# Keys of rows 2 and 3: the last half chunk as 64-row matmul pairs in a joint visit

## The chip, the cores and the metric

The kernel runs on one core of a Trainium2 chip. The metric is the time of one execution on the device in microseconds (us), as the median of several executions. "PE" is the tensor engine, "PEld" its weight loads, DVE the vector engine, ACT the scalar engine, POOL the GpSimd engine and SP the sync engine that issues most transfers.

## The reference

Two branches read the same x (2048 tokens, 448 features) and are mixed by a gate per token:

```python
qkv = x @ wqkv                       # 16 heads of 28
phi(t) = concat(softmax(t @ w_phi), softmax(-(t @ w_phi)))   # for q and k
kv, z = phi(k)^T v, sum phi(k)
a = (phi(q) kv / (phi(q) z + 1e-6)) @ wo
b = gelu(x @ w1 + b1) @ w2 + b2
out = g * a + (1 - g) * b            # g = sigmoid(sum(x * gate_w))
```

What matters here is the keys, `x @ Wpk`, where Wpk is the key weight already multiplied by w_phi. The 448 features are three chunks of 128 and half a chunk of 64.

## The kernel before

`xT` holds x transposed: features on partitions, tokens along the row. A tile is 128 tokens, a key pair (the "row" of the change's name) is two tiles. The fourth chunk is loaded as features 320 to 447, and the weight is zero in the first 64 partitions of that chunk. So it is a full 128-row matmul for 64 useful features:

```python
def k_pair(u, b1=False):                 # keys of tiles 2u, 2u+1
    pk = four("pk")
    for i in range(2):
        for c in range(NC4):             # 4 chunks, the last one half empty
            nc.tensor.matmul(pk[:, i, 0:D], lhsT=xT[:, c, tile], rhs=Wpk[:, c, :], ...)
    if b1:                               # a tiny matmul that turns b1 onto partitions
        nc.tensor.matmul(pk[:, 1, 480:480 + NJ], lhsT=b1c, rhs=ident[:, 0:NJ], ...)
    k_exp(u, pk)                         # two exponentials on ACT, PSUM -> phik
    if b1: nc.scalar.copy(out=b1T[:], in_=pk[:, 1, 480:480 + NJ])

# order                                   # POOL copies
k_pair(0); k_pair(1); k_norm(0)           # WvS <- WvG, halves swapped (2 copies)
k_pair(2); k_norm(1)                      # WkS[0:64]   <- Wpk[64:128]
k_pair(3, b1=True)                        # WkS[64:128] <- Wpk[0:64]
v_both()                                  # x1o <- xT[64:128, 3, 512:1024]
for g in range(NG): q_pair(g, 0)
for r in range(4): k_two(r); v_two(r); ...; q_pair(r, 1)
```

The values of rows 2 and 3 (`v_both`) avoid the waste already: their last chunk is computed from two places at once, one tile from partitions 0 to 63 (through the shifted copies `x1o` and `WvS`), the other from partitions 64 to 127. `k_two` does all its chunks so. For that it reads `xS`, a copy of x with the partition halves swapped, which transfers fill (`swap_x`). `four()` hands out PSUM buffers, three in turn plus a fourth.

The softmax here doesn't subtract the row's maximum and nothing guards it: scores larger than these inputs give would overflow.

Of the kernel before, what the change touches and what calls it, by code (L numbers as in the profile page):

```python
# [13 lines left out]
D = 448  # L14
# [3 lines left out]
P = 128  # L18
# [10 lines left out]
HP = 64  # L29
# [6 lines left out]
def kernel(  # L36
# [14 lines left out]
    nc = tc.nc  # L51
# [9 lines left out]
    def pair(name):  # L61
        return ps.tile([P, 2, 512], F32, name=name, tag="pair", bufs=3)

    def wide(name):
        return ps.tile([P, 2, 512], F32, name=name, tag="acc", bufs=1)
# [3 lines left out]
    def four(name):  # L69
        turn[0] += 1  # L70
        return wide(name) if turn[0] % 4 == 0 else pair(name)


    xT = consts.tile([P, NC4, S], BF16, name="xT")
# [23 lines left out]
    WvG = attn.tile([P, NC4, D + 1], BF16, name="WvG")  # L98
    WvS = attn.tile([P, NC4, D + 1], BF16, name="WvS")
    WkS = attn.tile([P, NC4, D], BF16, name="WkS")  # L100
    Wpk = attn.tile([P, NC4, D], BF16, name="Wpk")
# [38 lines left out]
    def swap_x(h, part=None):  # L140
        ev = slice(2 * h * 512, 2 * h * 512 + 512)
        od = slice(2 * h * 512 + 512, 2 * h * 512 + 1024)
        if part != "odd":
            nc.sync.dma_start(xS[0:HP, :, h, :], xT[HP:P, :, ev])
        if part != "even":
            nc.sync.dma_start(xS[HP:P, 0:3, h, :], xT[0:HP, 0:3, od])
# [29 lines left out]
                          in_=mask[:, PW:PW + 2, None].to_broadcast([P, 2, DH]))  # L176
    nc.gpsimd.memset(KVbd[:], 0.0)
    for g in range(NG):
        nc.gpsimd.tensor_copy(
            out=KVbd[:, g].rearrange("p s (i w) -> p s i w", i=2)[:, :, :, KW - 2:KW],  # L180
            in_=m4[:, None, :, :].to_broadcast([P, 2, 2, 2]))
# [11 lines left out]
    def copy(on_act, out, in_):  # L193
        if on_act:
            nc.scalar.copy(out=out, in_=in_)
        else:
            nc.vector.tensor_copy(out=out, in_=in_)  # L197

    def v_out(u, v_ps, tiles, on_act=False):
        copy(on_act, vaug[:, 2 * u:2 * u + 2, :, 0:PW],  # L200
             v_ps[:, :, 0:D].rearrange("p i (x d) -> p i x d", x=NPR))
        copy(on_act, lg[:, tiles], v_ps[:, :, D])
# [7 lines left out]
                                 rhs=WvG[:, c, :], start=(c == 0), stop=(c == NC4 - 1))  # L210
        v_out(u, v_ps, slice(2 * u, 2 * u + 2), on_act)

    def v_both():
        vs = [four("v_ps"), four("v_ps")]
        for m in range(2):
            for i in range(2):
                t = 4 + 2 * m + i
                for c in range(3):
                    nc.tensor.matmul(vs[m][:, i, 0:D + 1], lhsT=xT[:, c, t * P:(t + 1) * P],  # L219
                                     rhs=WvG[:, c, :], start=(c == 0), stop=False)  # L220
        for i in range(2):
            nc.tensor.matmul(vs[0][:, i, 0:D + 1], lhsT=x1o[:, i * P:(i + 1) * P],  # L222
                             rhs=WvS[0:HP, 3, :], start=False, stop=True)
            nc.tensor.matmul(vs[1][:, i, 0:D + 1], lhsT=xT[HP:P, 3, (6 + i) * P:(7 + i) * P],
                             rhs=WvG[HP:P, 3, :], start=False, stop=True)
        for m in range(2):
            v_out(2 + m, vs[m], slice(4 + 2 * m, 6 + 2 * m))

    def prep(W_T, out_at, engines):
        for m in range(2):  # L230
# [33 lines left out]
    def k_exp(u, pk):  # L264
        tt = slice(2 * u, 2 * u + 2)
        src = pk[:, :, 0:D].rearrange("p i (x w) -> p i x w", w=PW)
        nc.scalar.activation(out=phik[:, tt, :, 0, 0:PW], in_=src, func=ACT.Exp)  # L267
        nc.scalar.activation(out=phik[:, tt, :, 1, 0:PW], in_=src, func=ACT.Exp, scale=-1.0)  # L268

    def k_norm(u):  # L270
        tt = slice(2 * u, 2 * u + 2)
        sums = work.tile([P, 32, 2], F32, name="sums", bufs=3)
        ph = phik[:, tt].rearrange("p t x s w -> p (t x s) w")[:, :, 0:PW]
        ph = ph.rearrange("p y (h d) -> p y h d", d=DH)
        nc.vector.reduce_sum(out=sums[:], in_=ph, axis=AX.X)  # L275
        rec = work.tile([P, 32, 2], F32, name="rec", bufs=3)
        nc.vector.reciprocal(out=rec[:], in_=sums[:])  # L277
        parts = [(nc.gpsimd, 0, 32)] if u < 7 else [(nc.vector, 0, 16), (nc.gpsimd, 16, 32)]
        for eng, lo, hi in parts:
            eng.tensor_tensor(out=ph[:, lo:hi], in0=ph[:, lo:hi],  # L280
                              in1=rec[:, lo:hi, :, None].to_broadcast([P, hi - lo, 2, DH]),
                              op=ALU.mult)

    def k_pair(u, b1=False):
        pk = four("pk")
        for i in range(2):
            t = 2 * u + i
            for c in range(NC4):
                nc.tensor.matmul(pk[:, i, 0:D], lhsT=xT[:, c, t * P:(t + 1) * P],  # L289
                                 rhs=Wpk[:, c, :], start=(c == 0), stop=(c == NC4 - 1))  # L290
        if b1:
            nc.tensor.matmul(pk[:, 1, 480:480 + NJ], lhsT=b1c, rhs=ident[:, 0:NJ],
                             start=True, stop=True, skip_group_check=True)
        k_exp(u, pk)
        if b1:
            nc.scalar.copy(out=b1T[:], in_=pk[:, 1, 480:480 + NJ])
# [89 lines left out]
    def swap_w(W_S, W):  # L386
        nc.sync.dma_start(W_S[0:HP, :, :], W[HP:P, :, :])
        nc.sync.dma_start(W_S[HP:P, 0:3, :], W[0:HP, 0:3, :])

    def swap_on_pool(W_S, W):  # L390
        nc.gpsimd.tensor_copy(out=W_S[0:HP, :, :], in_=W[HP:P, :, :])
        nc.gpsimd.tensor_copy(out=W_S[HP:P, 0:3, :], in_=W[0:HP, 0:3, :])

    nc.gpsimd.dma_start(b1c[0:NJ, :], B_b1.rearrange("(j p) -> j p", p=P))
    x1o = oT[0:HP, 1, 0:512]
    swap_on_pool(WvS, WvG)
    swap_on_pool(WkS, Wpk)
    nc.gpsimd.tensor_copy(out=x1o, in_=xT[HP:P, 3, 512:1024])
    swap_x(0, "even")
    swap_w(WqS, Wpq)  # L400
    swap_x(0, "odd")
# [9 lines left out]
    nc.sync.dma_start(wo_sb[64:65, 3, :], B_b2[None, :])  # L411

    k_pair(0)
    k_pair(1)
    k_norm(0)
    k_pair(2)
    k_norm(1)
    k_pair(3, b1=True)
    v_both()
    nc.sync.dma_start(w2_sb[:], B_w2.rearrange("(j p) n -> p j n", p=P))  # L420
    k_norm(2)
# [148 lines left out]
```

## Time and profile before

| | kernel before |
|---|---|
| median of the first three runs | 155.75 us (155.66 to 155.77) |
| span of the profiled execution | 153.4 us |
| PE busy | 149.4 us, 97% |
| first key matmul to first query matmul | 8.87 us (11.13 to 20.00) |

PE is busy without a gap from the weight preparation to its last matmul, 2.95 us before the end, so the time is the sum of PE's matmuls, plus any wait for something with a date of its own. The prediction shows the lines.

### The profile page before, as it was taken

To read this page: it belongs to the slowest core of one execution; us is meant where nothing else is said; L and a number is where in the kernel's file an instruction comes from. 1 tells how busy PE (TensorE), PEld (TensorE's weight loads), DVE (VectorE), ACT (ScalarE), POOL (GpSimd) and SP (SyncE) were. 2 spreads that over 40 slices of the span, in tenths; PEclk is the share of its full clock that TensorE was granted. 3 is DMA by queue.
4 is the path that set the end of the run, shared out by engine and by line. 5 is a ranking of instruction groups with operands and counts; after the bars stand their busy time and mean duration, and the time that the engine had idled before them with its cause. 6 is when DMAs were issued, how large, how long until landed. Compare 5 with 4: busy or idle time off the path is not lost.

```text
span 153.4 us, 3189 instructions
## 1 busy us (share of the span) xinstructions
PE 149.4 (97%) x1302; PEld 79.8 (52%) x1302; DVE 83.0 (54%) x244; ACT 77.3 (50%) x93; POOL 39.8 (26%) x41
## 2 busy tenths in 40 slices
PE   7999999999999999999999999999999999999992
PEld 2675544444544854444444455555556555555561
DVE  3444989499890050000000059999977999977100
ACT  2569949999889437676777740111311111111112
POOL 7999796949874000000000000000000000000000
PEclk9999999999999999999999999999999999999999
DMA  4996998999990000000000001124332123334411
GB/s 149 235 214 150 215 168 195 231 221 218 232 368 23 4 0 4 0 0 4 0 0 0 4 0 34 34 44 93 94 94 64 41 64 91 74 94 38 109 45 30
DMA packets 27922, 14.11 MB, mean 92 GB/s; under 512 B 19842, under 2 KB 27780, under 8 KB 27908
## 3 DMA queue, kind: packets, MB, share of 16 engines
q1 hardware_dynamic: 26692, 13.25, 38.9%
q10 hardware_dynamic: 1152, 0.65, 1.6%
q8 instruction: 10, 0.16, 0.5%
q14 instruction: 4, 0.03, 0.1%
q0 software_dynamic: 64, 0.01, 0.0%
HBM read 6.11 MB, written 1.84 MB: 52 GB/s over the span
## 4 chain that ended last, share of the span: by engine, by line
PE 97%; ACT 0%; issue 0%; DVE 0%; ACTq 0%
PE y L509 28%; PE hp L450 28%; PE y L515 8%; PE pq L324 8%; PE nm L465 4%; PE pk L289 4%; PE v_ps L308 3%; PE pk L316 3%; PE acc L335 2%; PE v_ps L209 2%; PE warm_ps L371 2%; PE v_ps L219 2%; PE w_ps L236 1%; PE xp L354 1%; PE v_ps L222 0%; ACT res L518 0%
## 5 line engine op out<-in xcount | busy, mean ns | idle before, releaser
L509 PE MATMUL y<-w_sb,gel 128*128 128x448 bf16 (+2 forms) x238 | 45.2, 341 | 0.0
L450 PE MATMUL hp<-xT,w_sb 64*128 64x512 bf16 x196 | 42.6, 376 | 0.0
L450 PE MATMUL hp<-xS,w_sb 64*128 64x512 bf16 x196 | 42.6, 376 | 0.0
L455 ACT ACTIVATE gel<-hp,b1T 128x1024 bf16<-128x1024 f32 x28 | 30.8, 1111 | 13.0 <-PE hp L450 13.0
L518 ACT ACTIVATE res<-y,ungate 128x448 bf16<-128x448 f32 (+2 forms) x17 | 10.4, 612 | 50.3 <-PE y L515 50.1
L509 PEld LDWEIGHTS <-gel 128*128 128x128 bf16 x238 | 22.6, 98 | 19.6
L450 PEld LDWEIGHTS <-w_sb 64*128 64x128 bf16 x392 | 19.0, 94 | 23.0
L280 POOL TENSOR_TENSOR phik<-phik,rec 128x1792 bf16<-128x1792 bf16 (+1 forms) x8 | 24.9, 3128 | 6.5 <-DVE rec L277 6.5
L470 DVE COPY st<-nm 128x32 f32<-128x32 f32 x32 | 4.5, 183 | 35.6 <-PE nm L465 35.6
L486 DVE TENSOR_TENSOR tmp<-nm,al 128x448 bf16<-128x448 f32 x32 | 18.4, 615 | 0.0
L275 DVE TENSOR_REDUCE sums<-phik 128x64 f32<-128x1792 bf16 x8 | 16.0, 2000 | 2.7 <-ACT phik L268 2.7
L515 PE MATMUL y<-wo_sb,oT 128*128 128x448 bf16 (+2 forms) x68 | 14.7, 342 | 0.0
L324 PE MATMUL pq<-xT,Wpq 64*128 64x512 bf16 x56 | 12.9, 376 | 0.0
L324 PE MATMUL pq<-xS,WqS 64*128 64x512 bf16 x56 | 12.9, 376 | 0.0
L329 ACT ACTIVATE EqP<-pq 128x1024 bf16<-128x1024 f32 x8 | 8.4, 1049 | 3.8 <-PE pq L324 3.8
L197 DVE CAST vaug<-v_ps 128x896 bf16<-128x896 f32 x7 | 7.5, 1081 | 4.7 <-PE v_ps L209 2.1
L330 ACT ACTIVATE EqN<-pq 128x1024 bf16<-128x1024 f32 x8 | 8.4, 1052 | 0.0
L465 PE MATMUL nm<-KVbd,EqP 128*128 128x120 bf16 x64 | 8.3, 216 | 0.0
L465 PE MATMUL nm<-KVbd,EqN 128*128 128x120 bf16 x64 | 8.3, 216 | 0.0
L267 ACT ACTIVATE phik<-pk 128x896 bf16<-128x896 f32 x8 | 7.7, 957 | 0.3 <-PE pk L289 0.3
L515 PEld LDWEIGHTS <-oT 128*128 128x128 bf16 x68 | 6.0, 98 | 3.5
L268 ACT ACTIVATE phik<-pk 128x896 bf16<-128x896 f32 x8 | 7.7, 967 | 0.0
(102 smaller groups left out, 160.7 us busy)
## 6 DMA issues: line engine op xcount, KB each, us to landing
w_sb<-in_B_w_dram SPq DMA_DIRECT2D x4, 784.0 KB, 11.4
out_dram<-res SPq DMA_DIRECT2D x15, 112.0 KB, 1.9
w_sb<-in_B_w_dram SPq DMA_DIRECT2D x1, 1568.0 KB, 17.1
xS<-xT SPq DMA_DIRECT2D x2, 256.0 KB
oT<-in_A_x_dram ACTq DMA_DIRECT2D x1, 448.0 KB, 3.2
xS<-xT SPq DMA_DIRECT2D x2, 192.0 KB, 3.0
wo_sb<-in_A_wo_dram SPq DMA_DIRECT2D x1, 336.0 KB
WqS<-Wpq SPq DMA_DIRECT2D x1, 256.0 KB, 3.2
```

What stands on the lines that cost most here:

```text
L275: nc.vector.reduce_sum(out=sums[:], in_=ph, axis=AX.X)
L280: eng.tensor_tensor(out=ph[:, lo:hi], in0=ph[:, lo:hi], in1=rec[:, lo:hi, :, None].to_broadcast([P, hi - lo, 2, DH]), op=ALU.mult)
L324: nc.tensor.matmul(pq[:, i, :], lhsT=w_half(Wpq, WqS, i, k)[:, g * P:(g + 1) * P], rhs=x_half(i, k, h), start=(k == 0), stop=(k == NK - 1))
L329: nc.scalar.activation(out=EqP[:, g, dst], in_=src, func=ACT.Exp)
L330: nc.scalar.activation(out=EqN[:, g, dst], in_=src, func=ACT.Exp, scale=-1.0)
L450: nc.tensor.matmul(hp[:, i, :], lhsT=w1_sb[i * HP:(i + 1) * HP, k, j * P:(j + 1) * P], rhs=x_half(i, k, h), start=(k == 0), stop=(k == NK ...
L455: nc.scalar.activation(out=gel[h][:, j, :], in_=hp[:].rearrange("p a b -> p (a b)"), func=ACT.Gelu_apprx_tanh, bias=b1T[:, j:j + 1])
L465: nc.tensor.matmul(nm[s][:, g * 2 * KW:(g + 1) * 2 * KW], lhsT=E[:, g, tok], rhs=KVbd[:, g, s, :], start=True, stop=True)
L486: nc.vector.tensor_tensor(out=tmp[:, s, :].rearrange("p (x h d) -> p x h d", x=NPR, h=2), in0=nmv[s][:, :, 0:PW].rearrange("p x (h d) -> p ...
L509: nc.tensor.matmul(y, lhsT=gel[t // 8][:, j, (t % 8) * P:(t % 8 + 1) * P], rhs=w2_sb[:, j, cols], start=(j == 0), stop=False)
L515: nc.tensor.matmul(y, lhsT=oT[:, c, tok], rhs=wo_sb[:, c, cols], start=False, stop=(c == NC4 - 1))
L518: nc.scalar.activation(out=res[:, cols], in_=y, func=ACT.Copy, scale=ungate[:, t:t + 1])
```

## The change

The intent is to let the keys of rows 2 and 3 do what the values of these rows do: 12 full-row matmuls and two concurrent pairs of 64-row ones, in place of 16 full-row ones. Both rows' buffers must then be open together, so it is a visit of its own (`k_both`). The b1 matmul moves to the second key pair. On POOL the copy of x that the pairs need is moved ahead of the key weight's second half.

```diff
-    def v_both():
-        vs = [four("v_ps"), four("v_ps")]
+    def both(name, W, W_S, n):
+        pair_ps = [four(name), four(name)]
         for m in range(2):
             for i in range(2):
                 t = 4 + 2 * m + i
                 for c in range(3):
+                    nc.tensor.matmul(pair_ps[m][:, i, 0:n], lhsT=xT[:, c, t * P:(t + 1) * P],
+                                     rhs=W[:, c, :], start=(c == 0), stop=False)
         for i in range(2):
+            nc.tensor.matmul(pair_ps[0][:, i, 0:n], lhsT=x1o[:, i * P:(i + 1) * P],
+                             rhs=W_S[0:HP, 3, :], start=False, stop=True)
+            nc.tensor.matmul(pair_ps[1][:, i, 0:n], lhsT=xT[HP:P, 3, (6 + i) * P:(7 + i) * P],
+                             rhs=W[HP:P, 3, :], start=False, stop=True)
+    # v_both() and k_both() call both() and evict (cut)
@@
-    swap_on_pool(WkS, Wpk)
+    nc.gpsimd.tensor_copy(out=WkS[0:HP, :, :], in_=Wpk[HP:P, :, :])
     nc.gpsimd.tensor_copy(out=x1o, in_=xT[HP:P, 3, 512:1024])
+    nc.gpsimd.tensor_copy(out=WkS[HP:P, 0:3, :], in_=Wpk[0:HP, 0:3, :])
@@
     k_pair(0)
-    k_pair(1)
+    k_pair(1, b1=True)
     k_norm(0)
-    k_pair(2)
+    k_both()
     k_norm(1)
-    k_pair(3, b1=True)
     v_both()
```

More of the change, by code (lines that the diff above doesn't have):

```diff
@@ L218, in v_both, with k_both @@
                 for c in range(3):
-                    nc.tensor.matmul(vs[m][:, i, 0:D + 1], lhsT=xT[:, c, t * P:(t + 1) * P],
-                                     rhs=WvG[:, c, :], start=(c == 0), stop=False)
+                    nc.tensor.matmul(pair_ps[m][:, i, 0:n], lhsT=xT[:, c, t * P:(t + 1) * P],
+                                     rhs=W[:, c, :], start=(c == 0), stop=False)
         for i in range(2):
-            nc.tensor.matmul(vs[0][:, i, 0:D + 1], lhsT=x1o[:, i * P:(i + 1) * P],
-                             rhs=WvS[0:HP, 3, :], start=False, stop=True)
-            nc.tensor.matmul(vs[1][:, i, 0:D + 1], lhsT=xT[HP:P, 3, (6 + i) * P:(7 + i) * P],
-                             rhs=WvG[HP:P, 3, :], start=False, stop=True)
-        for m in range(2):
-            v_out(2 + m, vs[m], slice(4 + 2 * m, 6 + 2 * m))
+            nc.tensor.matmul(pair_ps[0][:, i, 0:n], lhsT=x1o[:, i * P:(i + 1) * P],
+                             rhs=W_S[0:HP, 3, :], start=False, stop=True)
+            nc.tensor.matmul(pair_ps[1][:, i, 0:n], lhsT=xT[HP:P, 3, (6 + i) * P:(7 + i) * P],
+                             rhs=W[HP:P, 3, :], start=False, stop=True)
+        return pair_ps
+    def v_both():
+        for m, v_ps in enumerate(both("v_ps", WvG, WvS, D + 1)):
+            v_out(2 + m, v_ps, slice(4 + 2 * m, 6 + 2 * m))
+    def k_both():
+        for m, pk in enumerate(both("pk", Wpk, WkS, D)):
+            k_exp(2 + m, pk)
     def prep(W_T, out_at, engines):
```

## The prediction

> **What bounds the kernel now.** I read the page first, then the chain of work that ended last in order of time, then the timelines of the tensor engine, its weight loads, ACT, POOL and the DMA issues between 11 and 31 us, which is where the diff acts and where its effects meet the next stage.
>
> ```profile
> PE 149.4 (97%) x1302; PEld 79.8 (52%) x1302; DVE 83.0 (54%) x244; ACT 77.3 (50%) x93; POOL 39.8 (26%) x41
> PE 97%; ACT 0%; issue 0%; DVE 0%; ACTq 0%
> ...
> 11.30 6.05 PE pk L289 x32
> 17.35 0.01 PE pk L292
> 17.36 2.31 PE v_ps L219 x12
> 19.67 0.29 PE v_ps L222
> ...
> 20.16 6.04 PE pq L324 x56
> 26.21 1.32 PE pk L316 x14
> ```
>
> The first two lines are busy times and shares of the chain by engine: 97% of the chain is matmul. The rest is that chain in time (start, length, what). The keys of rows 0 to 3 are the 32 matmuls at L289, 6.05 us or 0.189 us each. The values of rows 2 and 3 follow (L219, then half-row pairs L222/L224), then the queries (L324), then the first key visit of the upper half (L316). No gap on PE: each matmul taken out is worth 0.189 us, **unless** something later is waiting for a date that PE doesn't set.
>
> So I looked for such dates. Start, length, engine, line, what it does, from the timelines:
>
> ```profile
> 12.66 1.68 POOL L391 COPY WkS<-Wpk 64x1792 bf16<-64x1792 bf16 x1
> 14.38 1.30 POOL L392 COPY WkS<-Wpk 64x1344 bf16<-64x1344 bf16 x1
> 15.74 0.61 POOL L398 COPY oT<-xT 64x512 bf16<-64x512 bf16 x1
> ...
> 19.24 0.25 ACT L296 COPY b1T<-pk 128x14 f32<-128x14 f32 x1
> 21.72 1.02 ACT L329 ACTIVATE EqP<-pq 128x1024 bf16<-128x1024 f32 x1 [2.22 <-PE pq L324]
> ...
> 19.60 0.09 PEld L222 LDWEIGHTS <-oT 64*128 64x128 bf16 x1 [0.37 <-issue]
> ...
> 23.10 0.59 SPq L146 DMA_DIRECT2D xS<-xT  x1
> DMA to landing us min/median/max: 2.8/2.8/2.8
> ...
> 25.83 0.09 PEld L316 LDWEIGHTS <-xT 64*128 64x128 bf16 x1
> 25.93 0.21 PEld L316 LDWEIGHTS <-xS 64*128 64x128 bf16 x2
> ...
> 30.00 0.09 PEld L316 LDWEIGHTS <-xT 64*128 64x128 bf16 x1
> 30.00 0.31 PEld L316 LDWEIGHTS <-xS 64*128 64x128 bf16 x2
> ```
>
> The last six lines matter most. The second partition swap of x (issued at 23.10, landing 2.8 us later, so at 25.9) fills the half of xS that the first upper-half key visit loads as weights. In the steady visits (30.00) the xT load and the xS load start together. In the first visit the xS load starts 0.10 later, at 25.93, just after the landing. The matmuls lost almost nothing (26.04 and 26.05), since a weight is loaded about 0.2 us ahead. PE meets this transfer **with no slack at all**.
>
> **What the Trainium skill says.** (1) "TensorE: Matmul & The Clock Gate", section "Wait — 56ns, not 53.3ns?": warm back-to-back matmuls start N / 2.4 GHz + about 2.5 ns apart. For 448 columns that is 189 ns; the trace has 6.05 / 32 = 0.189 us. It agrees. The durations of 352 ns in the trace are not the price. (2) Same page, "Part 3: Packing small matmuls — row/col tiling": matmuls in different row groups run concurrently. The trace agrees: L222 and L224 both start at 19.61 and again both at 19.81. (3) "TensorEngine Tiling (Array Packing)", section "Key Properties": "Mode switching requires drain". The trace agrees: before L222 the weight load sat idle for 0.37 us, and the first pair starts at 19.61 although the last full-row matmul started at 19.32 (19.13 + 0.19) and the next slot was 19.51. So entering half-row mode cost 0.10 us. Leaving it is seen where L450 hands over to the 128-row L335: last pair at 50.06, slot 0.216, due at 50.28, started at 50.37, so 0.09 us. (4) "DMA: Bandwidth & Descriptors", section "Why a DMA increments its semaphore by 16 and not by 1": a transfer is done when all its engines have reported. The trace agrees so far as it shows a consumer released 0.03 us after the landing.
>
> **The change part by part.**
>
> Tensor engine. The keys of rows 2 and 3 (tiles 4 to 7) are 16 full-row matmuls now: 16 x 0.189 = 3.02 us. Afterwards there are 12 full-row ones (three whole chunks for four tiles), 12 x 0.189 = 2.27, and four half-row ones in two concurrent pairs, 2 x 0.19 = 0.38. The visit of the values that follows begins with full-row matmuls, so both switches are paid: 0.10 to enter and 0.09 to leave. Sum 2.84. Saved on PE: 3.02 - 2.84 = **0.18 us**; of the ideal two slots, 0.38, half goes into switches. The 64-row form suffices because the last chunk of the weight is zero in its first 64 partitions, by the kernel's own memset. The b1 matmul (14 columns, about 0.03 us of chain) only moves from the fourth key pair to the second.
>
> POOL. The same three copies in another order: 1.68, then 0.61 for the x half (from 14.38 to about 15.0), then 1.30 (to about 16.3). The end is the same as now (16.35), so the first normalise on POOL at 17.39 keeps its date. The new pairs need the first copy and the x half at about 14.15 + 12 x 0.189 = 16.4; they are there at 15.0, 1.4 us early. In the old order the x half would be there only at 16.35, with no slack: that is what the reorder is for. The third copy is needed at 26.
>
> b1. Its DMA is issued by POOL at 9.0 and lands 3.1 us later, at 12.1; the matmul that reads it will now stand at about 14.1 rather than 17.2. Two us to spare.
>
> ACT. The exponentials of pairs 0 and 1 run until 16.05, then the b1T copy (0.25) until 16.3. Pair 2 can now start only when the joint visit is done, about 17.2, where it started at 16.05; so pairs 2 and 3 end about 20.5 rather than 19.2. ACT has the room: it idled 2.22 us before the first query exponential (21.72). Buffers: the second query group needs the buffer of pair 3 at about 21.3, and has it at about 20.5. The first query group needs that of pair 2 at 19.8, and has it at 18.8. No PE wait follows.
>
> The sum at the next date. PE reaches the first upper-half key visit 0.18 us earlier, so its xS load would be due at about 25.65. The landing doesn't move with PE: the swap is issued when the transposed loads of x have landed, those are issued by the sync queue behind swaps that depend on weight preparation before 13 us, and none of that is touched. So the load again starts at 25.93 and its matmul at about 26.03 or 26.05. PE waits 0.16 to 0.18 us there, and the gain is **0.00 to 0.02 us**. After that visit the chain is the same instructions at full PE occupancy, so the rest keeps its length.
>
> **The rivals.** *Gain stays whole.* If in a typical execution the swap lands 0.2 us earlier against PE than in this trace, the 0.18 us come through: 155.57 us. For it: one trace is one draw of DMA timing; against it: the page's DMA row shows the DMA engines nearly always busy up to there, so little makes them earlier. *ACT becomes the bound.* ACT is continuous from 21.72 to 34 us, with 1.8 us per query group against 1.51 on PE, and it starts that stretch from idle; if the later exponentials ran into it, query groups would wait for buffers and the time rise by up to 0.3, to 156.0. Against it: 20.5 is still 1.0 us before the first query result. *A switch costs more than I read off.* If each were 0.2 us, the joint key visit would save nothing; the result is 155.75 again, not distinguishable from the DMA by time but plainly so in the trace. *DVE or POOL late:* the third and fourth normalise start at 22.34 and 24.85, well after the exponentials; I give that no weight.
>
> **Range and chances.** From 155.75 I take 0.05: the central estimate of the DMA case (0.01) mixed with about one chance in four that the swap lands early enough to let 0.18 through. That is 155.70 us. The three runs of the kernel before spread over 0.11 us, and two builds may differ by something like that for no reason in the diff; so 155.40 to 155.95. A change of 2% is 3.1 us; all parts together are a tenth of that, so "same" is nearly certain.
>
> **What would show it.** Right, if in the changed kernel's trace (a) the stretch from the first full-row matmul of the joint key visit to the first of the values' visit is about 2.84 us; (b) the query groups start about 0.18 us earlier, near 19.8; (c) the first xS weight load of the upper half is still at about 25.9, with a wait before it of about 0.2 us and its releaser a DMA; (d) later stages, as the first gelu layer matmul (42.72) and the end, have the old dates. Wrong, if the first xS load moves forward by the whole 0.18, or if PE waits for POOL at the first pair or for ACT at a query group.

## The result, and the profile after

The changed kernel took 155.45 us (median of 6 runs, 155.13 to 155.64), the kernel before 155.70 us in the same rounds and the earlier ones (6 runs, 155.43 to 155.83). The ratio is 0.9983, with a 95% interval of 0.9970 to 0.9996.

The page of the changed kernel, busy times and then the engines' shares of the last chain:

```profile
PE 148.8 (97%) x1302; PEld 78.6 (51%) x1302; DVE 83.1 (54%) x244; ACT 77.4 (50%) x93; POOL 39.6 (26%) x41
PE 91%; DMA 3%; SPq 2%; issue 0%; DVE 0%; ACT 0%; ACTq 0%
```

The number of matmul instructions is the same, since four full-row ones became four half-row ones. The 3% of DMA in the chain is at the start: in this execution the weight preparation met a late transfer of the query weights, at 10.2 us. That is before the changed part. The chain of waits in order of time (start, length, what):

```profile
11.29 3.03 PE pk L296 x16
14.32 0.01 PE pk L299
14.33 2.29 PE pk L219 x12
16.61 0.29 PE pk L222
...
17.10 2.40 PE v_ps L219 x12
...
19.99 6.04 PE pq L331 x56
26.03 1.32 PE pk L323 x14
```

Against the lines of before: the query groups (L331, formerly L324) begin at 19.99 instead of 20.16, and the first upper-half key visit (L323, formerly L316) at 26.03 instead of 26.21. The 0.17 us is there, and it isn't lost at that visit. The timelines of the changed kernel, for PE, its weight loads, POOL, ACT and the transfer issues:

```profile
14.18 2.43 PE L219 MATMUL pk<-Wpk,xT 128*128 128x448 bf16 x12
16.55 0.36 PE L222 MATMUL pk<-WkS,oT 64*128 64x448 bf16 x1
16.75 0.35 PE L222 MATMUL pk<-WkS,oT 64*128 64x448 bf16 x1
17.03 2.47 PE L219 MATMUL v_ps<-WvG,xT 128*128 128x449 bf16 x12
...
17.03 2.03 PEld L219 LDWEIGHTS <-xT 128*128 128x128 bf16 x12 [0.37 <-issue]
...
14.16 0.61 POOL L405 COPY oT<-xT 64x512 bf16<-64x512 bf16 x1
...
17.13 0.92 ACT L274 ACTIVATE phik<-pk 128x896 bf16<-128x896 f32 x1 [0.88 <-PE pk L224]
21.54 1.02 ACT L336 ACTIVATE EqP<-pq 128x1024 bf16<-128x1024 f32 x1 [1.07 <-PE pq L331]
...
22.72 0.59 SPq L146 DMA_DIRECT2D xS<-xT  x1
DMA to landing us min/median/max: 2.8/2.8/2.8
...
25.66 0.09 PEld L323 LDWEIGHTS <-xT 64*128 64x128 bf16 x1
25.66 0.31 PEld L323 LDWEIGHTS <-xS 64*128 64x128 bf16 x2
```

The joint visit is 17.03 - 14.18 = 2.85 us instead of 3.02. The weight loads pause for 0.37 us on leaving the half-row mode, as they do on entering it. ACT starts the third pair's exponentials at 17.13 instead of 16.05 and still idles 1.07 us before the first query group. The swap was issued at 22.72, not at 23.10, and landed at 25.5 instead of 25.9. The xS load was not held up.

### The profile page after: what moved, and what is told of

It reads as the page before. It is cut to its first block, busy times and chain, and to the rows that moved or that the text cites. A ratio compares the mean times of both kernels' runs of the same rounds, so it can differ in the third digit from the quotient of the medians.

```text
span 153.2 us, 3189 instructions
## 1 busy us (share of the span) xinstructions
PE 148.8 (97%) x1302; PEld 78.6 (51%) x1302; DVE 83.1 (54%) x244; ACT 77.4 (50%) x93; POOL 39.6 (26%) x41
## 4 chain that ended last, share of the span: by engine, by line
PE 91%; DMA 3%; SPq 2%; issue 0%; DVE 0%; ACT 0%; ACTq 0%
PE hp L457 28%; PE y L516 28%; PE y L522 8%; PE pq L331 8%; PE nm L472 4%; PE v_ps L315 3%; PE pk L323 3%; DMA WqT<-in_A_wqkv_dram 3%; PE acc L342 2%; PE pk L296 2%; SPq L138 2%; PE v_ps L219 2%; PE pk L219 1%; PE w_ps L243 1%; SPq L126 1%; PE v_ps L222 0%
## 5 line engine op out<-in xcount | busy, mean ns | idle before, releaser
L331 PE MATMUL pq<-xT,Wpq 64*128 64x512 bf16 x56 | 12.9, 376 | 0.0
L331 PE MATMUL pq<-xS,WqS 64*128 64x512 bf16 x56 | 12.9, 376 | 0.0
```

The lines of the kernel that those rows point to most:

```text
L331: nc.tensor.matmul(pq[:, i, :], lhsT=w_half(Wpq, WqS, i, k)[:, g * P:(g + 1) * P], rhs=x_half(i, k, h), start=(k == 0), stop=(k == NK - 1))
```

## The experiments

The theory after this result was: the pairs save two slots of 0.189 us (a slot is the time from the start of one matmul to the next) less one switch into half-row mode and one out, and the date of the swap is a draw of each execution (a matter of chance) that mostly leaves room. The rivals were: the regrouping or the POOL order brings the gain; the new order itself moves the swap; the switches cost nothing and something else limits the gain. All results below were correct. They were taken on three chips: the second look of the changed kernel, full rows, the order and the old POOL order on one, the late and early swaps on another, and the rest on a third. Each set was compared with runs of the kernel before in the same rounds.

The next table is made from the profiles. "Stretch" is the start of the first query matmul less that of the first key matmul. "Due" is the start of the first upper-half xT weight load, with which the xS load starts when nothing holds it. "Landing" is the date in the trace at which the second swap's second half had reported completely. All in us.

| profile | first key matmul | stretch | due | landing | xS load |
|---|---|---|---|---|---|
| before | 11.13 | 8.87 | 25.83 | 25.89 | 25.93 |
| before, second look | 10.99 | 8.87 | 25.69 | 25.43 | 25.69 |
| full rows in the joint visit | 11.15 | 8.86 | 25.84 | 25.75 | 25.85 |
| only the order changed | 11.39 | 8.91 | 26.12 | 26.13 | 26.18 |
| two visits | 10.99 | 8.91 | 25.73 | 25.64 | 25.73 |
| old POOL order | 10.88 | 8.82 | 25.53 | 25.42 | 25.53 |
| changed | 11.13 | 8.70 | 25.66 | 25.49 | 25.66 |
| changed, second look | 11.31 | 8.74 | 25.88 | 25.82 | 25.88 |
| changed, third look | 10.77 | 8.70 | 25.30 | 25.44 | 25.48 |
| rows 0 and 1 too | 11.45 | 8.53 | 25.81 | 25.95 | 25.99 |

In all ten, the first xS matmul starts 6.05 us after the first query matmul: PE lost nothing at the swap in any of them. What follows, to the end of PE's work, is equal within 0.01 us as well. So up to the end of PE's work, profiles of these kernels differ in two numbers only: when the first key matmul starts (10.77 to 11.45, set by the stages before it) and the stretch. After PE's last matmul come 2.94 to 2.96 us more in nine of them, and 3.32 us in "rows 0 and 1 too". The stretch of one kernel repeats within 0.04 us: in the second look of the changed kernel and in "only the order changed", the fourth key matmul starts 0.23 us after the third instead of 0.19.

### The changed kernel again, second and third look

> The changed kernel once more, for a second draw of its transfers and more timed runs. Theory (the two slots less two switches are saved on PE, and come through when the second swap of x lands before PE wants it): PE again reaches the first query matmul near 19.83 us if the weight preparation ends at the same date; the ratio to the kernel before is between 0.9983 and 1.000, nearer 0.9988 (0.18 us of 155.7). If the landing is later than about 25.65 in this profile, a wait of PE before the first xS weight load takes its place. Rival (the new order itself moved the transfers earlier, worth another 0.1 us or more): the landing is again at about 25.5 and not near 25.9.

> The changed kernel for a third time, beside the two above. Theory: stretch from the first key matmul to the first query matmul 8.70 to 8.74 us, no wait at the first xS load, ratio 0.9988 within the interval. The start of the key visit (11.13 and 11.31 us in the earlier two profiles) sets the rest of the difference between executions.

The second set gave 155.40 us against 155.37 (ratio 0.9993, interval 0.9977 to 1.0009), the third 155.47 against 155.41 (0.9997, 0.9981 to 1.0013). Each interval holds both 0.9989, which 0.17 us would make, and 1.000. The mean of the three ratios is 0.9991, or 0.14 us. The stretch was 8.74 and 8.70. The rival "the new order moves the swap" falls: the landing was at 25.82 in the second look. The third look tells more. The weight loads of the changed kernel in its third look, then its matmuls at that place:

```profile
25.30 0.09 PEld L323 LDWEIGHTS <-xT 64*128 64x128 bf16 x1
25.48 0.12 PEld L323 LDWEIGHTS <-xS 64*128 64x128 bf16 x2
...
25.51 0.35 PE L323 MATMUL pk<-Wpk,xT 64*128 64x448 bf16 x1
25.51 0.54 PE L323 MATMUL pk<-WkS,xS 64*128 64x448 bf16 x2
```

PE came early (first key matmul at 10.77), and the swap, landing 0.14 us after the xS load was due, held that load for 0.18 us. The two matmuls start at 25.51 all the same, where the steady pace puts them. A matmul that starts 0.03 us after its weight load began is enough, so almost the whole lead of 0.21 us of the loads is slack.

### The kernel before, second look

> The kernel before, for a second look. Theory: stretch 8.87 to 8.91 us. The landing of the second swap in the first profile (25.89, just 0.04 us before the load that needs it) was a late draw: the load is now due at least 0.05 us after the landing. Rival (the kernel before always meets it exactly): within 0.05 us again.

One run, 155.32 us; it serves for its dates alone. The transfer issue and the weight loads of the kernel before in its second look:

```profile
22.66 0.59 SPq L146 DMA_DIRECT2D xS<-xT  x1
...
25.69 0.09 PEld L316 LDWEIGHTS <-xT 64*128 64x128 bf16 x1
25.69 0.31 PEld L316 LDWEIGHTS <-xS 64*128 64x128 bf16 x2
```

The swap went out at 22.66 instead of 23.10 and landed 0.26 us before it was wanted. The theory's condition holds: the late landing isn't a property of the kernel before. Whether the first look differs by the execution alone or also by its chip is not shown, since the kernel before was not profiled twice on one chip. On the chip of the second look of the changed kernel, the landing came 14.51 to 14.74 us after the first key matmul in four kernels.

### Full rows in the joint visit

```diff
-        for m, pk in enumerate(both("pk", Wpk, WkS, D)):
+        # as k_pair: all four chunks on 128 rows, for both pairs, then the exponentials
+        for m in range(2):
+            for i in range(2):
+                for c in range(NC4): nc.tensor.matmul(pks[m][:, i, 0:D], ..., rhs=Wpk[:, c, :])
```

> The joint visit of the keys of rows 2 and 3, but with all 16 matmuls on full rows; everything else as in the changed kernel. Theory: the gain is the half-row pairs alone, so this is 0.17 to 0.20 us slower than the changed kernel on PE: joint visit 3.02 us, first query matmul near 20.0, ratio to the kernel before 1.000. Rival (the regrouping, the b1 move or the order of copies gives the gain): ratio near 0.998 and the first query matmul near 19.83.

155.63 us against 155.37, ratio 1.0014 (0.9999 to 1.0028). The chain of waits of this kernel:

```profile
14.35 3.04 PE pk L238 x16
17.39 2.30 PE v_ps L219 x12
```

The visit takes 3.04 us and the stretch is back at 8.86. Visit, order and b1 move are as in the changed kernel; only the pairs are gone, and the gain with them.

### Only the order changed

```diff
     k_norm(0)
-    k_both()
+    k_pair(2)
     k_norm(1)
+    k_pair(3)
     v_both()
```

> The kernel before with only the new order of POOL copies and the b1 matmul moved to the second key pair. Theory: nothing on PE's chain changes, first query matmul near 20.0, ratio 1.000. Rival (POOL's new order shifts the swap transfers): landing of the second swap near 25.5 rather than 25.9, and ratio below 0.9995.

155.52 us against 155.37, ratio 1.0008 (0.9994 to 1.0022). The stretch is 8.91 and the landing at 26.13, the latest of all. Neither the copies' new order nor the b1 move helps, and they don't bring the swap forward.

### The old POOL order

```diff
-    nc.gpsimd.tensor_copy(out=WkS[0:HP, :, :], in_=Wpk[HP:P, :, :])
+    swap_on_pool(WkS, Wpk)
     nc.gpsimd.tensor_copy(out=x1o, in_=xT[HP:P, 3, 512:1024])
-    nc.gpsimd.tensor_copy(out=WkS[HP:P, 0:3, :], in_=Wpk[0:HP, 0:3, :])
```

> The changed kernel with POOL's copies in the old order, so that the x half is copied last and ready at about 16.35 us, where PE's first half-row load wants it at about 16.45 to 16.55. Theory: no wait or one of under 0.1 us; ratio to the kernel before 0.9985 to 0.9995, first query matmul 19.83 to 19.95. Rival (the reorder is what makes the change work): PE waits 0.2 us or more before the first half-row pair, first query matmul at 20.0 or later, ratio 1.000 or above.

155.23 us against 155.37, ratio 0.9989 (0.9973 to 1.0004), so the time tells nothing. The trace does. POOL's last copy and PE's first half-row weight load with the old order:

```profile
15.76 0.61 POOL L405 COPY oT<-xT 64x512 bf16<-64x512 bf16 x1
...
16.42 0.09 PEld L222 LDWEIGHTS <-oT 64*128 64x128 bf16 x1 [0.49 <-POOL oT L405]
```

The load starts 0.05 us after the copy ends and waited 0.49 us instead of the 0.37 of a bare switch. The stretch is 8.82: 0.12 us of the 0.17 is given back. That is a little over the 0.1 us that the theory allowed and under the 0.2 of the rival. PE was early here (10.88) while POOL's dates hardly moved, so by these dates the amount would be smaller where PE starts later; in the changed kernel the copy ends at 14.77, some 1.8 us early.

### Two visits, one pair each

```diff
-    k_both()
+    k_split(2)      # 6 full-row matmuls, then one half-row pair (tiles 4 and 5)
     k_norm(1)
+    k_split(3)      # the same for tiles 6 and 7
```

> The half-row pairs in two visits, one pair each (tiles 4 and 5, then tiles 6 and 7), so that PE enters and leaves the half-row mode twice for the same two slots saved; the copies that the first pair needs come first on POOL. Theory (a switch in and out costs 0.19 us together, as much as one slot): the stretch from the first key matmul to the first query matmul is 8.70 + 0.19 = 8.89 us, no better than the 8.87 of the kernel before; ratio 1.000. Rival (a switch is hidden, and the gain of 0.17 us is limited by something else): 8.70 us or less, ratio 0.999.

155.64 us against 155.41, ratio 1.0013 (0.9999 to 1.0028). PE's timeline with two visits:

```profile
14.04 1.29 PE L237 MATMUL pk<-Wpk,xT 128*128 128x448 bf16 x6
15.27 0.36 PE L239 MATMUL pk<-WkS,oT 64*128 64x448 bf16 x1
15.56 1.31 PE L237 MATMUL pk<-Wpk,xT 128*128 128x448 bf16 x6
16.81 0.36 PE L239 MATMUL pk<-WkS,oT 64*128 64x448 bf16 x1
17.10 2.47 PE L219 MATMUL v_ps<-WvG,xT 128*128 128x449 bf16 x12
```

Six full-row slots after 14.04 end at 15.17 (6 x 0.189 = 1.13), and the pair starts at 15.27, so entering costs 0.10. The pair's own slot ends at 15.46 and the next full-row matmul starts at 15.56, so leaving costs 0.10. The stretch is 8.91, against 8.89 expected: two slots saved, four switches paid, nothing left. This is why the pairs of both rows are done in one visit.

### The swap made later

```diff
-    swap_x(1)
+    swap_x(1, "even")
+    nc.sync.dma_start(wo_sb[:, 0:3, :], ...)     # moved up from below
+    swap_x(1, "odd")
```

This edit was made in the kernel before and in the changed kernel.

> The kernel before, with the 336 KB load of the output weights put between the two halves of the second swap of x, so that the swap's second half lands about 1 to 1.7 us later (near 27). No work is added. Theory of the date that PE doesn't set: PE waits for this landing before its first xS weight load, about 1.0 us, and the time rises by as much, ratio about 1.006. Rival (the swap has slack in most executions, or PE catches up): no rise.

> The changed kernel with the same late swap. Theory: PE arrives 0.17 us earlier at the same landing and waits longer by that, so this and the kernel before with the late swap take the same time within 0.1 us apart from the draw of the landing, and the wait on PE is about 1.2 us. Rival (the change's gain is independent of the swap): 0.17 us or more faster than the kernel before with the late swap.

The kernel before with it took 156.97 us against 155.78 (ratio 1.0084, 1.0055 to 1.0112), the changed one 157.12 (three fast runs; 1.0083, 1.0058 to 1.0109). The weight loads of the kernel before with the late swap, and the matmul that waited:

```profile
25.91 0.09 PEld L316 LDWEIGHTS <-xT 64*128 64x128 bf16 x1
27.68 0.10 PEld L316 LDWEIGHTS <-xS 64*128 64x128 bf16 x2 [1.68 <-DMA xS<-xT]
...
27.68 0.36 PE L316 MATMUL pk<-WkS,xS 64*128 64x448 bf16 x2 [1.22 <-DMA xS<-xT]
```

So the wall that the prediction argued from does exist: the swap took 4.6 us from issue, landed at 27.64, and PE waited for it. The matmul starts 7.61 us after the first query matmul instead of 6.05, so PE lost about 1.6 us; the 1.0 us and the ratio of 1.006 expected were too small, because the swap landed later than the 27 us assumed. The matmul is recorded at the same 27.68 as its weight load. The two ratios agree with the change being worth nothing there, but they are too coarse to exclude the 0.0011 of the gain.

### The swap made earlier

```diff
     swap_x(0, "even")
+    load_x(2, "wide")
     swap_w(WqS, Wpq)
     swap_x(0, "odd")
-    load_x(2)
+    load_x(2, "rest")
     load_x(3)
```

> The kernel before, with the first transposed load of the third x block issued in the 1.4 us in which the sync queue waits for the weight preparation, ahead of the query weights' swap. The second swap of x should land 0.7 to 1.5 us earlier (24.4 to 25.2), the query weights' swap somewhat later. Theory: the kernel before met the swap with no loss, so ratio 1.000 unless some of its executions have a later landing than its profile; then up to 0.001 lower. A wait at the first query visit would show the query weights late.

> The changed kernel with the earlier swap. Theory: the gain on PE no longer depends on the draw: 0.17 to 0.2 us faster than the kernel before with the early swap, ratio to the kernel before 0.998 to 0.9988, and no wait before the first xS load. Rival (query weights late): a wait at the first query matmul, ratio 1.000 or above.

The kernel before with it took 155.70 us (ratio 1.0009, 0.9972 to 1.0046), the changed one 155.71 (0.9998, 0.9979 to 1.0016). The second swap did land earlier (25.24 and 25.25), but the first swap's second half, which is now issued behind the load moved ahead of it, took 4.9 and 4.5 us instead of 3.1 and landed at 20.2 instead of about 18. PE's timeline of the changed kernel with the early swap:

```profile
19.78 0.38 PE L331 MATMUL pq<-xT,Wpq 64*128 64x512 bf16 x1
20.29 0.39 PE L331 MATMUL pq<-xS,WqS 64*128 64x512 bf16 x2
```

The queries start at 19.78, and their second matmul, which belongs beside the first, starts at 20.29, 0.04 us after that landing at 20.25. PE lost 0.5 us, more than the change had saved. In the kernel before with the same edit the first query matmul came at 20.25, just after the landing, and lost nothing. This is the effect that was predicted for the changed kernel at the other swap: a gain on PE that runs into a transfer with its own date. It was made by moving a transfer, and it doesn't occur in the changed kernel itself. The edit is no improvement, and the gain of 0.17 to 0.2 us expected for it did not come; the wait is at the first query group, as the rival said, but for the swap of x and not for the query weights.

### Rows 0 and 1 too

```diff
-    k_pair(0)
-    k_pair(1, b1=True)
+    k_both(0)       # last chunk of tiles 0, 1 from x0o, a POOL copy; of tiles 2, 3 in place
     k_norm(0)
-    k_both()
+    k_both(4)
```

POOL makes `x0o` first, and the quarter of `WkS` that the pairs need before the rest of it. The b1 matmul follows the first visit's pairs.

> Rows 0 and 1 get a joint visit with half-row pairs too, with a copy of the last chunk of their x by POOL and the copies that each visit needs in front. Theory: two more slots less two more switches, so the stretch from the first key matmul to the first query matmul is 8.70 - 0.17 = 8.53 us, and 0.17 us less in time than the changed kernel unless the second swap of x is met late; its landing came 0.06 to 0.17 us before PE wanted it in the two profiles of the changed kernel, so a wait of 0 to 0.1 us is possible there. Ratio to the kernel before 0.9975 to 0.9985. Rival (ACT, whose exponentials begin 1.3 us later, becomes the bound): a wait of PE at the second query group or later, ratio 0.999 or above.

155.26 us against 155.41, ratio 0.9985 (0.9971 to 0.9999). PE's timeline of the first joint visit, then ACT's:

```profile
11.45 2.43 PE L220 MATMUL pk<-Wpk,xT 128*128 128x448 bf16 x12
13.81 0.36 PE L223 MATMUL pk<-WkS,oT 64*128 64x448 bf16 x1
...
14.40 0.92 ACT L280 ACTIVATE phik<-pk 128x896 bf16<-128x896 f32 x1 [1.54 <-PE pk L225]
21.70 1.02 ACT L342 ACTIVATE EqP<-pq 128x1024 bf16<-128x1024 f32 x1 [0.64 <-PE pq L337]
```

The stretch is 8.53, as expected. ACT starts its exponentials at 14.40 and still idles 0.64 us before the first query group, so the ACT rival doesn't come true. The swap held the xS load for 0.18 us (due 25.81, load 25.99), which the lead of the loads hid once more. In the traces the stretch of this version is 0.17 us shorter than that of the changed kernel and 0.34 us shorter than that of the kernel before (8.87 - 8.53); its profiled execution as a whole was not shorter (153.7 us), since it began its keys late and ended late. By its timed runs it is faster than the kernel before within its interval (0.9971 to 0.9999), while against the changed kernel of the same rounds (155.47) the timed runs don't settle it. It has the shortest stretch of the versions tried.

## Why the prediction was right or wrong

The measured 155.45 us lies inside the range of 155.40 to 155.95, close to its lower end; the central 155.70 was 0.25 too high. That it lies inside is owed to the width of the range, so to luck: the central case rests on a step that failed. Of the signs that the prediction named, (a) and (b) came. (c) and (d) did not: the first xS load moved from 25.93 to 25.66 and had no wait before it, which the prediction had named as a sign of being wrong, and the first gelu layer matmul moved with it, from 42.72 to 42.55.

- **The change's worth on PE** was right. The joint visit was put at 2.84 us and measured 2.85; the saving at 0.18 and measured 0.17; the query groups at 19.8 and measured at 19.83. The cost of the switches, read from two other places of the old trace, held: two visits with four switches save nothing.
- **POOL, b1 and ACT** were right. The x half was ready at 14.77 (put at 15.0), the third pair's exponentials started at 17.13 (put at 17.2), and no wait of PE followed. That the old order of copies would leave no slack was shown: 0.12 us was lost with it in its profile.
- **"The sum at the next date" was the step that failed.** It said that the landing doesn't move with PE, that the load "again starts at 25.93 and its matmul at about 26.03 or 26.05", and that the gain would be 0.00 to 0.02 us. The runs put two things in its place. First, 25.89 was one draw and a late one: measured from the first key matmul, the landing came between 14.36 and 14.75 us later in the ten profiles, and the kernel before's first look was the latest, with "only the order changed" beside it. Second, I took it that the matmul follows its weight load by at least 0.1 us. A lead of 0.03 was enough, and with the late swap load and matmul are both at 27.68; so a landing 0.14 us after the due date, with the load 0.18 us late, cost nothing. The prediction had this lead before it ("a weight is loaded about 0.2 us ahead") and still wrote "no slack at all". By an estimate from these figures, the first look's own landing would have cost 0.05 to 0.08 us and not 0.16 to 0.18: matmul at 25.93 to 25.96, against 26.05 - 0.17 = 25.88 at full gain.
- **The rival "gain stays whole"** came true. I gave it about one chance in four. Its number, 155.57, takes the 0.17 us off the earlier median. The other 0.1 us of the first comparison is not shown to be the change's: the second and third gave 0.9993 and 0.9997, and the start of the key visit alone varies by 0.68 us. That the change is faster at all rests on the stretches; the timed runs of the second and third set alone don't show it.
- **The rivals of ACT and of dearer switches** were rightly put low.

## What to carry to other kernels

A half-row pair saves a slot, but going into and out of half-row mode costs about one slot of 448 columns (0.19 us both here), so collect several pairs behind one switch. Before a transfer's date is called a wall, look at it in several executions, and count the lead of the weight loads as slack. When a change is worth a tenth of a per cent, compare stretches inside the traces, since the start of the kernel varies by more than that.

## What the Trainium skill lacked or had wrong

- "TensorEngine Tiling (Array Packing)", section "Key Properties", says that a mode switch drains the engine but gives no size. Here it was 0.10 us going in and 0.09 to 0.10 us coming out, for 128-row and 64-row matmuls of 448 and 449 columns, with the weight loads paused for 0.37 us before 16.54 and 17.03 in the changed kernel.
- "TensorE: Matmul & The Clock Gate", section "Architectural detail: the array is 16× 32×32, not 1× 128×128", says that a matmul can begin before its weight load completes. The runs agree, and they add what follows for waits: in the third look the xS load, which takes 0.09 us, started 0.18 us late and the matmul 0.03 us after it, on time.
- No page has how much the date of a transfer varies between executions. The swap's time from issue to landing was the same (2.7 to 2.8 us in five profiles of the two kernels), but its issue, behind a chain of other transfers, varied from 22.66 to 23.10 us in two profiles of the same kernel.
